# Norms, denominators and turns as single items between products; folds on ScalarE, q and k loaded from ScalarE's queue, pieces of x issued later

## The chip, the cores and the metric

The kernel runs on 1 core of a Trainium2 chip. A core has five engines with an instruction stream each: TensorE (PE in the profile; its weight loads are PEld), VectorE (DVE), ScalarE (ACT), GpSimd (POOL) and SyncE (SP), which here only issues DMAs. ScalarE issues DMAs too (rows named ACTq), from the same stream as its arithmetic. The metric is device time in microseconds (us) of the slowest core; here there is one.

## The reference

Everything is float32. Attention runs on 8 batches of 12 heads, sequence 448, head width 64; its output, with the heads side by side, is the input x of a token and channel mixer.

```python
def rmsnorm(x, g):
    rms = np.sqrt(np.mean(x * x, axis=-1, keepdims=True) + 1e-06)
    return x / rms * g
q_n, k_n = (rmsnorm(q, g_q), rmsnorm(k, g_k))
scores = scale * np.matmul(q_n, k_n.transpose(0, 1, 3, 2))
scores = scores - np.max(scores, axis=-1, keepdims=True)
attn = np.exp(scores)
attn = attn / (np.sum(attn, axis=-1, keepdims=True) + 1e-09)
x = np.matmul(attn, v)          # (8, 12, 448, 64) -> (8, 448, 768)
...
h = np.maximum(x.transpose(0, 2, 1) @ w_tok1, 0.0) @ w_tok2   # 448 -> 256 -> 448
u = x + h.transpose(0, 2, 1)
h2 = np.maximum(u @ w_ch1, 0.0) @ w_ch2                       # 768 -> 1536 -> 768
return u + h2
```

## The kernel before, in words

**Two bodies.** The product of the two gains decides at run time whether scores can be exponentiated without subtracting their maximum. The measured inputs take that body (`shifted` is false); the other is not run.

**Attention.** Two heads make a pair, six pairs a batch, 48 pairs in all; two pairs make a t, so a batch has three t. Each t has four steps, s = 0 to 3 (`att_step`). Item `tiled` of a step holds scores for one or two of seven key blocks k (L321, with one exp per pair on ScalarE, L325, from four PSUM banks s_ps), and the products with v of earlier blocks (L395, into two banks o_ps). Step 0 also finishes the t before: its last two blocks, and then `denominator` for its two pairs. For the first batch (pairs 0 to 5) the row sums are matmuls with ones (L375) into m_ps; later they are sums of the exps on POOL and VectorE (`group_sums`, L363) and one small matmul into d_ps.

`denominator` is four VectorE instructions for a pair: transpose the sums (L422), reciprocal of one column in 32 (L424), transpose back (L426), multiply o_ps into uT, the transposed x (L428).

**Norms.** q and k of a pair are squared on ScalarE (L1000, or L1005 for pairs below 12) and summed on VectorE (L1001, L1008) into ms. `roots` turns the sums of two pairs into reciprocal roots: for pairs from 12 on the two halves of a head width lie on different partitions, so four copies (L1027, the fold) and one sum (L1028) come first; then a first guess (L1036) and three Newton steps of three instructions (L1039 to L1041). `scale` multiplies q and k by them (L286, one a pair), and `turn_qk` transposes: with matmuls for pairs below 12 (`plain`, L298), otherwise on VectorE (L301); ScalarE applies the gains (L304). The buffer of q and k is one of two slots (qk_t); pair p + 2 overwrites pair p once that is turned. For pairs from 12 on, `load_qk` issues eight DMAs a pair (L983), all on SP.

**The mixer.** `tok1` (L565) needs x with the sequence on partitions. For the first batch matmuls transpose uT; for the others `trans_x` transposes a 128-column piece on VectorE into one of four buffers `turned` (`turn`, L523), sends it with four DMAs to a scratch xs in memory (`send`, L529, on SP), and after three pieces loads half of x from there (L556, on SP). `tok2` (L573) has its result added to uT by VectorE (L578). The channel products (`ch1`, L695; `ch2`, L752) go through PSUM banks m_ps, of which there are two; seven products replace eight, with sums on VectorE, POOL and ScalarE: of each seven, product i = 4 (and i = 0) is copied out by ScalarE, the others are taken out by VectorE (L700, L761). At the batch's end `turns` transposes uT again on VectorE and sends it to the output with four DMAs a piece on ScalarE's queue (L529).

**Weights.** They arrive as 8-byte numbers. `weight_items` converts them chunk by chunk (three VectorE instructions L213, L214, L216, two on ScalarE, one VectorE L233, one POOL L247) and stores them to scratch memory (ws); `sum_items` add the sums that the seven products need, on POOL. Products read units of weights from there (`load_units`, L621, on SP, six buffers, four or five ahead).

**The order.** Every engine's instructions are issued in the order in which the program is written (a manual schedule). Work is a list of items, each a planned cost in us and a function; `merge` interleaves two lists so that both are through by the same share of their planned cost at any time. In the main loop a batch's mixer (`early`) is merged with the next batch's attention (`att_items`), with `x_items` (0.1 a piece) in it. Items of planned cost 0 follow their predecessor directly, with nothing between: for later batches these are the squares of a pair (steps 0 and 1), the roots, both scalings, the turns and the loads. A product is planned at 2.24.

**Kernel start.** `Start` loads pairs 0 and 1 and norms pair 0 before the branch; pair 1 follows after it, pairs 2 and 3 after the first scores.

Of the kernel before, what the change touches and what calls it, by code (L numbers as in the profile page):

```python
# [44 lines left out]
def whole(ctx, tc, shifted, pre, q, k, v, g_q, g_k, moe_w_tok1, moe_w_tok2, moe_w_ch1, moe_w_ch2, out):  # L45
# [66 lines left out]
    s_tile = lambda name: ps_S.tile([P, 512], F32, name=name, tag="S")  # L112

# [295 lines left out]
    def denominator(p):  # L409
        b, j = divmod(p, NPAIR)  # L410
        if j == 0:
            st["uT", b] = uT_pool.tile([P, NC, S], F32, name="uT")
        ps = st.pop(("d", p))

        dt = rd_pool.tile([P, S], F32, name="dt", tag="rd")
        if shifted:
            nc.vector.tensor_scalar(dt[:], ps[:, 0:S], 1e-9, None, ALU.add)
            src = dt[:]
        else:

            src = ps[:, 0:S]
        nc.vector.transpose(out=dt[:], in_=src)  # L422
        rc = pre.nt_pool.tile([P, NB], F32, name="rc")
        nc.vector.reciprocal(out=rc[:], in_=dt[:].rearrange("p (n c) -> p n c", c=32)[:, :, 0])  # L424
        rd = rd_pool.tile([P, S], F32, name="rd", tag="rd")
        nc.vector.transpose(  # L426
            out=rd[:].rearrange("p (n c) -> p n c", c=32), in_=rc[:].unsqueeze(2).to_broadcast([P, NB, 32]))
        nc.vector.tensor_tensor(out=st["uT", b][:, j, :], in0=st.pop(("o", p))[:, 0:S], in1=rd[:], op=ALU.mult)  # L428
        st.pop(("v", p))
# [3 lines left out]
    def att_step(g):  # L433
# [8 lines left out]
        def finish():  # L442
            if s == 0 and t:
                last = (p - 2, p - 1)
                for k in (NK - 2, NK - 1):
                    values(last, k)
            if live:
                for k in ((0,), (1, 2), (3, 4), (5, 6))[s]:
                    score(t, k)
            if s == 0 and t:  # L450
                if not on_pe(p - 1):
                    row_sums(t - 1)
                for i in last:
                    denominator(i)
# [16 lines left out]
        def both_shifted():  # L471
# [8 lines left out]
            denominator(i)  # L480
# [10 lines left out]
        items.append((2.4 if s == 1 else 3.2, tiled))  # L491
        if live and not on_pe(p):
# [6 lines left out]
        if live and s in (3, 0):  # L499
            j = p + 4 if s == 3 else p + 3  # L500
            if pre.first_slot + 2 <= j < NP:
                items.append((0.0, lambda: pre.load_qk(j, st)))

        n = p + 2
        if g in (0, 3):
            n = 2 if g == 0 else 4
            items += [(0.3, lambda i=i: pre.squares(n + i, st)) for i in range(2)]
        elif live and s < 2 and NPAIR <= n < NP:
            items.append((0.0, lambda: pre.squares(n + s, st)))
        if g in (0, 3) or live and s == 1 and NPAIR <= n < NP:  # L510
            items.append((0.3 * (n < NPAIR), lambda: pre.roots(n, 2, st)))
            items += [(0.3 * (n < NPAIR), lambda i=i: scale(n + i)) for i in range(2)]
        if turned and not inside:
            items += [(0.4 * pre.plain(q), lambda i=i: turn_qk(q, i)) for i in (1, 0)]
# [18 lines left out]
    def x_tile(half):  # L533
        st["x", half] = x_pool.tile([P, NS, HC], F32, name="x")
        return st["x", half]

    def trans_x(b, j):

        half, o = divmod(j * P, HC)
        if b == 0:  # L540

            if o == 0:
                x_tile(half)
            ps = s_tile("t_ps")
            for c in range(NS):
# [3 lines left out]
                out=st["x", half][0:R, :, o:o + P], in_=ps[0:R, :].rearrange("p (c n) -> p c n", c=NS))  # L549
# [4 lines left out]
        send(nc.sync, turn(b, j), xs[:, o:o + P])  # L554
        if o + P == HC:
            nc.sync.dma_start(out=x_tile(half)[0:R], in_=xs[:].rearrange("(c p) n -> p c n", c=NS))  # L556
            st.pop(("xs", half))

    def tok1(b, jc, h):
# [4 lines left out]
        for c in range(NS):  # L564
            nc.tensor.matmul(  # L565
                out=ps[:, 0:HC], lhsT=w1_sb[0:R, c, jc * P:(jc + 1) * P], rhs=st["x", h][0:R, c, :],
# [218 lines left out]

    def turns(b, cs):

        def trans(cc):
            st["y", b, cc] = turn(b, cc)

        def sent(cc):
            send(nc.scalar, st.pop(("y", b, cc)), out[b][:, cc * P:(cc + 1) * P])

        items = [(0.3, lambda cc=cc: trans(cc)) for cc in cs]
        late = [(0.3, lambda cc=cc: sent(cc)) for cc in cs]
        return items[:2] + [it for two in zip(late, items[2:]) for it in two] + late[max(0, len(cs) - 2):]
# [49 lines left out]
    scale(0)  # L846
    turn_qk(0, 1)
    turn_qk(0, 0)
    load_v(0)
    load_v(1)  # L850
    for i in range(5):
        weight_load(i)
        if i < NPAIR - 2:
            pre.load_qk(2 + i, st)
        if i < 2:
            load_v(2 + i)
    for i in range(2):
        pre.load_qk(pre.first_slot + i, st)

    pre.squares(1, st)  # L860
    pre.roots(1, 1, st)
    scale(1)
    turn_qk(1, 1)
    turn_qk(1, 0)
# [3 lines left out]
    for _, fn in merge(  # L868
            att_items(0, 8) + merge(att_items(8, AHEAD * per + 1), x_items(0, 0)), weight_items(0, BEFORE)):
        fn()  # L870
    left, sums = [], sum_items()
    for b in range(B):
# [5 lines left out]
        else:  # L878

            for _, fn in merge(tok1_items(b, 0), left):  # L880
                fn()
# [8 lines left out]
        for _, fn in merge(att, early[:len(early) - tail]) + early[len(early) - tail:] + last_items(b, sums[6:12]):  # L890
            fn()
        left = turns(b, [2, KC + 2])
    for _, fn in left:
        fn()


class Start:


    def __init__(self, ctx, tc, q, k, g_q, g_k, w2):  # L900
# [27 lines left out]
        self.load_qk(1, self.st)  # L928
# [12 lines left out]
        nc.gpsimd.memset(self.sq[:, :, D:D + 1], D * 1e-6)  # L941

# [3 lines left out]
        self.st["rs", 0] = const.tile([P, 4 * self.NS], F32, name="rs_0")[0:self.R]  # L946
# [164 lines left out]
```

## Time and profile before

| | us |
|---|---|
| median of 3 runs | 1449.41 |
| lowest, highest | 1445.63, 1452.39 |
| profiled execution, its own time | 1447.23 |
| its span in the profile | 1445.3 |
| TensorE busy in it | 1306.8 |
| VectorE, GpSimd, ScalarE busy | 783.0, 394.1, 368.6 |

The page gives busy times over the span, the span in 40 slices of 36.1 us (a digit is the busy share in tenths; PEclk is the clock granted to TensorE, in tenths of full speed), the chain of work that ended last, the costliest groups of instructions by line, and DMA issues. Views of the trace answer further questions: waits (who waited for whom: us in total, times, longest), the timeline (start, duration, engine, line, operation, output<-inputs, number of instructions, and in brackets the idle time before and what ended it), and tables by stretches of time. Names are the program's tiles: m_ps, s_ps, o_ps, d_ps are PSUM banks; hb is a large buffer that holds early q and k at first and the mixer's hidden values later.

### The profile page before, as it was taken

How to read it: one execution, taken by the hardware profiler on the slowest of the kernel's cores; microseconds unless marked ns; L12 is line 12 of the kernel's file. 1: busy time of each engine (PE TensorE's matmuls, PEld its weight loads, DVE VectorE, ACT ScalarE, POOL GpSimd, SP SyncE). 2: the span in 40 equal slices, each digit the busy share in tenths (PEclk: the TensorE clock that was granted, in tenths of full speed). 3: DMA queues.
4: the chain of work that ended last, by engine and by line, in shares of the span. 5: the costliest groups of instructions: out<-in, count | busy, mean ns of one | idle time of the engine just before them, and what ended most of it. 6: DMA issues, size and time to landing. Idle time of an engine off the chain costs nothing.

```text
span 1445.3 us, 20543 instructions
## 1 busy us (share of the span) xinstructions
PE 1306.8 (90%) x7408; PEld 933.5 (65%) x7408; DVE 783.0 (54%) x1382; ACT 368.6 (26%) x707; POOL 394.1 (27%) x385
## 2 busy tenths in 40 slices
PE   3777995998987899999999989999999999999997
PEld 1333442454666858786676847777587847787997
DVE  5767887435662545652656446562667446533312
ACT  3555453202231023311233013320323113210110
POOL 0112232515581222311133113220333113221220
PEclk9899998999997999999999999999999999999999
DMA  9255877795978845677356746588357746467455
GB/s 193 87 167 155 240 218 191 225 228 131 265 177 230 188 116 152 145 202 175 85 156 165 170 115 158 115 211 203 72 159 177 166 121 157 111 171 180 142 172 121
DMA packets 497396, 238.87 MB, mean 165 GB/s; under 512 B 375876, under 2 KB 455876, under 8 KB 497284
## 3 DMA queue, kind: packets, MB, share of 16 engines
q1 hardware_dynamic: 407138, 226.20, 59.5%
q10 hardware_dynamic: 90018, 11.25, 5.2%
q8 instruction: 61, 1.00, 0.3%
q14 instruction: 51, 0.42, 0.1%
q0 software_dynamic: 128, 0.00, 0.0%
HBM read 197.85 MB, written 39.52 MB: 164 GB/s over the span
## 4 chain that ended last, share of the span: by engine, by line
PE 66%; DVE 11%; DMA 11%; issue 3%; SPq 2%; ACT 1%; ACTq 1%; POOL 1%; DVEq 0%; POOLq 0%
PE m_ps L695 21%; PE m_ps L752 19%; PE o_ps L395 7%; PE s_ps L321 6%; DMA unit<-ws 4%; PE m_ps L573 4%; DMA out_dram<-turned 4%; PE m_ps L565 3%; PE m_ps L676 2%; PE m_ps L658 2%; DVE qk_t L286 2%; ACTq L529 1%; DMA ws<-raw 1%; DVE raw L214 1%; SPq L529 1%
## 5 line engine op out<-in xcount | busy, mean ns | idle before, releaser
L752 PE MATMUL m_ps<-hb,unit 128*128 128x224 f32 x1764 | 349.3, 359 | 35.2 <-DMA unit<-ws 33.7
L752 PEld LDWEIGHTS m_ps<-hb,unit 128*128 128x128 f32 x1764 | 336.2, 193 | 53.6 <-issue 33.6
L325 ACT ACTIVATE e<-s_ps 128x448 f32<-128x448 f32 x336 | 156.4, 547 | 199.0 <-PE s_ps L321 199.0
L695 PE MATMUL m_ps<-tu,unit 128*128 128x224 f32 x1008 | 203.0, 356 | 4.1 <-DVE r L700 4.1
L695 PEld LDWEIGHTS m_ps<-tu,unit 128*128 128x128 f32 x1008 | 190.2, 191 | 18.2 <-DVE r L700 8.8
L395 PE MATMUL o_ps<-e,v 64*64 64x448 f32 x1316 | 153.1, 547 | 6.6 <-DVE uT L428 5.7
L695 PEld LDWEIGHTS m_ps<-uT,unit 128*128 128x128 f32 x756 | 141.5, 190 | 18.9 <-issue 6.6
L695 PE MATMUL m_ps<-uT,unit 128*128 128x224 f32 x756 | 153.3, 356 | 0.0
L321 PE MATMUL s_ps<-qkT 64*64 64x448 f32 x1260 | 144.0, 550 | 0.5 <-ACT x L548 0.5
L761 POOL TENSOR_TENSOR uT<-uT,r 128x448 f32<-128x448 f32 (+1 forms) x56 | 59.3, 1069 | 279.0 <-DVE r L761 160.8
L761 DVE TENSOR_TENSOR uT<-uT,m_ps 128x448 f32<-128x448 f32 (+1 forms) x70 | 34.0, 502 | 137.6 <-PE m_ps L752 136.6
L573 PE MATMUL m_ps<-w_sb,h 128*128 128x448 f32 x192 | 86.4, 600 | 23.3 <-DVE uT L578 21.5
L363 DVE TENSOR_TENSOR es<-es,e 128x896 f32<-128x896 f32 x84 | 97.7, 1164 | 4.7 <-ACT e L325 2.2
L395 PEld LDWEIGHTS o_ps<-e,v 64*64 64x64 f32 x1316 | 49.4, 134 | 78.3 <-issue 66.3
L565 PE MATMUL m_ps<-x,w_sb 112*128 112x384 f32 x256 | 88.6, 497 | 2.9 <-ACT h L568 2.9
L304 ACT ACTIVATE qkT<-qkT,g_t 128x448 f32<-128x448 f32 x36 | 24.1, 669 | 261.7 <-DVE qkT L301 261.7
L321 PEld LDWEIGHTS s_ps<-qkT 64*64 64x64 f32 x1260 | 44.0, 133 | 68.8 <-issue 59.5
L363 POOL TENSOR_TENSOR es<-e 128x896 f32<-128x896 f32 x21 | 44.7, 2126 | 159.3 <-ACT e L325 159.3
L578 DVE TENSOR_TENSOR uT<-uT,m_ps 128x448 f32<-128x448 f32 x48 | 29.3, 616 | 103.0 <-PE m_ps L573 103.0
L700 POOL TENSOR_TENSOR hb<-r,r 128x448 f32<-128x448 f32 x21 | 23.8, 1134 | 223.8 <-ACT r L716 155.9
L573 PEld LDWEIGHTS m_ps<-w_sb,h 128*128 128x128 f32 x192 | 38.5, 210 | 68.8 <-issue 29.7
L247 POOL TENSOR_TENSOR stage<-raw 128x512 f32<-128x512 f32 x36 | 41.6, 1156 | 138.7 <-DVE raw L233 81.7
(92 smaller groups left out, 1426.2 us busy)
## 6 DMA issues: line engine op xcount, KB each, us to landing
unit<-ws SPq DMA_DIRECT2D x318, 384.0 KB, 3.6
raw<-in_moe_w_ch_dram SPq DMA_DIRECT2D x72, 256.0 KB, 3.6
out_dram<-turned ACTq DMA_DIRECT2D x192, 56.0 KB, 3.5
v<-in_v_dram SPq DMA_DIRECT2D x94, 112.0 KB, 3.5
xs<-turned SPq DMA_DIRECT2D x168, 56.0 KB, 1.9
x<-xs SPq DMA_DIRECT2D x14, 672.0 KB, 7.5
ws<-stage SPq DMA_DIRECT2D x36, 256.0 KB, 3.8
raw<-ws SPq DMA_DIRECT2D x36, 256.0 KB, 4.1
```

The costliest lines, as they stand in the source:

```text
L247: nc.gpsimd.tensor_tensor(out=dst, in0=lo, in1=hi, op=ALU.mult)
L286: nc.vector.tensor_tensor(out=x, in0=x, in1=r.unsqueeze(2).to_broadcast(list(x.shape)), op=ALU.mult)
L321: nc.tensor.matmul(out=pss[i][rows_of(i, a), 0:S], lhsT=qkT[h, 1, k * D:(k + 1) * D], rhs=qkT[h, 0, :], start=True, stop=True)
L325: nc.scalar.activation(out=e[:, i, :], in_=pss[i][:, 0:S], func=AF.Exp)
L363: eng.tensor_tensor(out=es[:], in0=(es if k > 1 else st["e", t, 0])[:], in1=st["e", t, k][:], op=ALU.add)
L395: nc.tensor.matmul(out=st["o", p][a * D:(a + 1) * D, 0:S], lhsT=vt[rows, k * D:(k + 1) * D], rhs=e[rows, :], **kw)
L565: nc.tensor.matmul(out=ps[:, 0:HC], lhsT=w1_sb[0:R, c, jc * P:(jc + 1) * P], rhs=st["x", h][0:R, c, :], start=(c == 0), stop=(c == NS - 1))
L573: nc.tensor.matmul(out=ps[:, 0:S], lhsT=st["h1", jc][:, cc * P:(cc + 1) * P], rhs=w2_sb[:, jc].rearrange("p c r -> p (c r)"), start=(jc == ...
L578: nc.vector.tensor_tensor(out=uT, in0=uT, in1=ps[:, 0:S], op=ALU.add)
L695: nc.tensor.matmul(out=ps[:, j * HS:(j + 1) * HS], lhsT=w[:, t, j, :], rhs=m, start=(t == 0), stop=(t == KC - 1))
L752: nc.tensor.matmul(out=ps[:, j * HS:(j + 1) * HS], lhsT=st["w"](j, t), rhs=hb[:, HB[what], t, :], start=(t == 0), stop=(t == KF - 1))
L761: add = lambda e, o, x, y: e.tensor_tensor(out=o, in0=x, in1=y, op=ALU.add)
```

## The change

- **A planned clock.** `run` adds up the planned cost of the items it executes; `later(us, fn)` puts a function off until that clock has advanced by us.
- **Denominators** become items of 0.4: transpose and reciprocal for both pairs, then transpose and product for both. For the first batch ScalarE copies o_ps to uT in between, and the product reads that copy.
- **Norms** become items of 0.4: square, reduce (both pairs at step 0, for t of 2 and more), then at step 1 fold, guess, three Newton steps, two scalings. The four copies of a fold run on ScalarE, after step 1's exps.
- **Turns** of q and k become items of 0.4 each, **loads** of q and k items of 0.2 for each DMA; for pairs from 12 on all eight DMAs of a pair are issued by ScalarE.
- **Pieces of x** are sent 2.0 planned us after their transposition, and the load of half of x stands 4.5 after the last of its three; **pieces of the output** are sent 2.0 after theirs.
- **Start:** pairs 0 and 1 share one norm before the branch, with the keys of pair 1, like those of pair 0, loaded by ScalarE; pairs 2 and 3 follow right after the branch. Pairs below 12 other than pair 0 are squared in one instruction, not in two halves.

The number of matmuls is the same (3764 in the program). ScalarE's DMAs go from 195 to 485, SP's from 1115 to 825; VectorE's copies from 72 to none, ScalarE's from 74 to 152.

```diff
+    clock, pending = [0.0], []
+    def later(us, fn):
+        pending.append((clock[0] + us, fn))
+    def run(items):
+        for c, fn in items:
+            fn()
+            clock[0] += c
+            while pending and pending[0][0] <= clock[0]:
+                pending.pop(0)[1]()
...
-    def denominator(p):
+    def denominators(ps):
+        def begin(p):
...
+            nc.vector.transpose(out=dt[:], in_=src)
+            st["rc", p] = rc = pre.nt_pool.tile([P, NB], F32, name="rc")
+            nc.vector.reciprocal(out=rc[:], in_=dt[:].rearrange("p (n c) -> p n c", c=32)[:, :, 0])
+        def raw(p):
+            b, j = divmod(p, NPAIR)
+            to = st["uT", b][:, j, :]
+            nc.scalar.copy(out=to, in_=st["o", p][:, 0:S])
+            st["o", p] = to
+        def end(p):
...
+            nc.vector.transpose(
+                out=rd[:].rearrange("p (n c) -> p n c", c=32),
+                in_=st.pop(("rc", p))[:].unsqueeze(2).to_broadcast([P, NB, 32]))
+            nc.vector.tensor_tensor(out=st["uT", b][:, j, :], in0=st.pop(("o", p))[:, 0:S], in1=rd[:], op=ALU.mult)
+        parts = [lambda p=p: begin(p) for p in ps]
+        if ps[0] < NPAIR:
+            parts += [lambda p=p: raw(p) for p in ps]
+        return parts + [lambda p=p: end(p) for p in ps]
...
         items.append((2.4 if s == 1 else 3.2, tiled))
+        part = lambda fns, c=0.4: [(c, fn) for fn in fns]
+        if s == 0 and t and not shifted:
+            items += part(denominators((p - 2, p - 1)))
...
-                items.append((0.0, lambda: pre.load_qk(j, st)))
-
-        n = p + 2
-        if g in (0, 3):
-            n = 2 if g == 0 else 4
-            items += [(0.3, lambda i=i: pre.squares(n + i, st)) for i in range(2)]
-        elif live and s < 2 and NPAIR <= n < NP:
-            items.append((0.0, lambda: pre.squares(n + s, st)))
-        if g in (0, 3) or live and s == 1 and NPAIR <= n < NP:
-            items.append((0.3 * (n < NPAIR), lambda: pre.roots(n, 2, st)))
-            items += [(0.3 * (n < NPAIR), lambda i=i: scale(n + i)) for i in range(2)]
+                eng = nc.sync if pre.plain(j) else nc.scalar
+                items += part(pre.loads(j, st, eng, eng), 0.2)
+        n = p + 2 if t > 1 else p + 4
+        if live and s == 1 - (t > 1) and t != 1 and n < NP:
+            items += part([lambda i=i, f=f: f(n + i, st) for i in range(2) for f in (pre.square, pre.reduce)])
+        if live and s == 1 and t != 1 and n < NP:
+            items += part(pre.roots(n, st)) + part([lambda i=i: scale(n + i) for i in range(2)])
         if turned and not inside:
-            items += [(0.4 * pre.plain(q), lambda i=i: turn_qk(q, i)) for i in (1, 0)]
+            items += part([lambda i=i: turn_qk(q, i) for i in (1, 0)])
...
-        send(nc.sync, turn(b, j), xs[:, o:o + P])
+        t = turn(b, j)
+        later(2.0, lambda: send(nc.sync, t, xs[:, o:o + P]))
         if o + P == HC:
-            nc.sync.dma_start(out=x_tile(half)[0:R], in_=xs[:].rearrange("(c p) n -> p c n", c=NS))
             st.pop(("xs", half))
+            later(4.5, lambda: nc.sync.dma_start(
+                out=x_tile(b, half)[0:R], in_=xs[:].rearrange("(c p) n -> p c n", c=NS)))
...
+    def trans_y(b, cc):
+        t = turn(b, cc)
+        later(2.0, lambda: send(nc.scalar, t, out[b][:, cc * P:(cc + 1) * P]))
     def turns(b, cs):
...
+        return [(0.3, lambda cc=cc: trans_y(b, cc)) for cc in cs]
...
+    pre.load_qk(2, st)
+    pre.load_qk(3, st)
     load_v(0)
     load_v(1)
...
+    scale(0)
+    pre.square(2, st)
+    for p in range(2):
+        if p:
+            scale(p)
+        turn_qk(p, 1)
+        turn_qk(p, 0)
+    pre.reduce(2, st)
+    pre.square(3, st)
+    pre.reduce(3, st)
+    for part in pre.roots(2, st):
+        part()
+    scale(2)
+    scale(3)
...
-        self.load_qk(1, self.st)
+        self.load_qk(1, self.st, other=nc.scalar)
...
+            for p in range(2):
+                self.square(p, self.st)
+                self.reduce(p, self.st)
+            for part in self.roots(0, self.st):
+                part()
...
+    def fold(self, p, st):
+        x = st["ms", p + 1].rearrange("p a n -> p (a n)")
+        st["half", p] = t = self.nt_pool.tile([128, 56], F32, name="half", tag="nt")
+        for m in range(4):
+            self.nc.scalar.copy(out=t[32 * m:32 * m + 32], in_=x[32 * (m ^ 1):32 * (m ^ 1) + 32])
...
+    def roots(self, p, st):
+        parts = [] if self.plain(p) else [lambda: self.fold(p, st)]
+        return parts + [lambda: self.guess(p, st)] + [lambda i=i: self.newton(p, st, i == 2) for i in range(3)]
```

`guess` holds L1028 and L1036 of before, `newton` one round of L1039 to L1041; `square` and `reduce` hold what `squares` held.

## The prediction

> **What bounds the kernel now.** I read the page first (busy shares, 40 slices), then TensorE's own waits, then the timeline around its longest gaps, the SP queue's waits and a table by stretches.
>
> ```profile
> PE 1306.8 (90%) x7408; PEld 933.5 (65%) x7408; DVE 783.0 (54%) x1382; ACT 368.6 (26%) x707; POOL 394.1 (27%) x385
> ...
> PE   3777995998987899999999989999999999999997
> ...
> DVE  5767887435662545652656446562667446533312
> ...
> PEclk9899998999997999999999999999999999999999
> ```
>
> TensorE is the bound: 1306.8 of 1445.3 us. What is left is 138.5 us: 12.6 before the first matmul, 9.1 after the last (it ends at 1436.2), and 117 in gaps between. The change touches no matmul, so it can win only from those 117 us and from half-clock stretches. TensorE's waits say what ends the gaps (us in total, times, longest):
>
> ```profile
> PE m_ps L752 <- DMA unit<-ws: 33.7, 11, 16.0
> PE m_ps L573 <- DVE uT L578: 21.5, 7, 5.1
> PE t_ps L298 <- DVE hb L286: 19.0, 2, 12.6
> PE m_ps L676 <- DMA unit<-ws: 16.4, 1, 16.4
> PE t_ps L298 <- issue: 8.6, 1, 8.6
> PE o_ps L395 <- DVE uT L428: 5.7, 2, 5.3
> ```
>
> Two causes: VectorE late (L573, L298, L395) and a unit of weights late (L752, L676). The first in the timeline of batch 2:
>
> ```profile
> 523.91 1.31 DVE L1027 COPY nt<-ms 32x56 f32<-32x56 f32 x4
> ...
> 527.99 2.10 DVE L286 TENSOR_TENSOR qk_t<-qk_t,rs 128x896 f32<-128x896 f32 x2
> 530.00 0.61 DVE L578 TENSOR_TENSOR uT<-uT,m_ps 128x448 f32<-128x448 f32 x1
> ...
> 530.67 4.49 PE L573 MATMUL m_ps<-w_sb,h 128*128 128x448 f32 x11 [2.28 <-DVE uT L578]
> ```
>
> One norm (reduce, folds, roots, two scalings) holds VectorE from 522.80 to 530.0; the eviction L578 is behind it, and TensorE idles 2.28 us. The second cause, at the end of that batch:
>
> ```profile
> 650.99 6.65 SPq L529 DMA_DIRECT2D xs<-turned  x12
> ...
> 657.74 1.49 SPq L621 DMA_DIRECT2D unit<-ws  x2
> 659.91 0.32 SPq L556 DMA_DIRECT2D x<-xs  x1
> ...
> 662.63 4.78 PE L752 MATMUL m_ps<-hb,unit 128*128 128x224 f32 x24 [1.59 <-DMA unit<-ws]
> ```
>
> SP issues twelve pieces of x, then a load of x that waits for them, and only then the unit TensorE waits for. SP also waits on ScalarE's stores:
>
> ```profile
> SPq L621 <- DMA out_dram<-turned: 52.3, 11, 8.4
> ```
>
> These data have nothing to do with each other: in the built program each DMA waits for the one eight places before it, over SP's and ScalarE's queues together. So a late DMA on one queue holds the other.
>
> **The change part by part.** The sum stands against the profiled execution, 1447.23 us (span 1445.3 and 1.9 around it); the median, 1449.41, lies 2.2 above.
>
> 1. Start. Before, pair 0 is turned from 12.59 and pair 1 from 20.72, scores begin at 22.41. Now both norms share one chain before the branch. Pair 1's keys go out on ScalarE right behind pair 0's (end near 3.1); with 4.7 us to landing (row hb<-in_q_dram) they are there at 7.8; squares 1.2, reduce 1.24, ten short steps of 32 columns 2.2 (30.34 to 32.55), branch 0.8, scaling 1.22: pair 0 turns at 14.5 (1.9 later), pair 1 one scaling and one turn later, scores at 18.3. Gain 4; ends 0 (a late landing) and 6.4 (the whole gap before 20.72). I take -4.5, as pairs 2 and 3 are normed before they are needed.
> 2. Rest of the start. Four gaps: 2.6 at 28.1, 4.5 at 33.8, 5.3 at 55.7, 8.6 at 88.4, together 21. For 55.7, the raw copy on ScalarE (row COPY 526 ns) frees o_ps without VectorE's 2.15 us of transposes, reciprocal and product per pair; but the denominators' m_ps still waits for VectorE behind a weight piece (3.0 us: 0.43+1.34+0.53+0.70). For 88.4, the norm of pairs 6 and 7 still stands one step before its turn. Half: -10, ends 0 and -21. VectorE's work is unchanged but for the folds.
> 3. The wait at 235 (16.4). The units there come at 248.26, behind 6.2 us of pieces of x (242.0 to 248.2) and 3.6 us of q and k. Now the three transposes stand before two weight pieces, and the q and k are on ScalarE; the pieces still precede the units. -5; ends 0 (the last weights are VectorE's, whatever SP does) and -10.
> 4. Norms at tok2 (L573, 21.5 in 7 waits). Folds leave VectorE (72 copies, 37.6 us); scalings come one by one between products. At a batch's start the order is now: roots 2.7, eviction 0.62, two scalings 2.2, eviction 0.62, beside two tok2 products (3.2) and 3.3 of scores and values. The waits should nearly go. Against it: the folds stand behind four exps (4 x 0.55) in ScalarE's queue, the root's first step behind them, and output DMAs (4 x 0.61, from four in 2.45 at 512.79) now stand right before these exps. ScalarE's price of a fold lies between 0.20 (128x1 activation) and 0.53 (128x448 copy), 0.8 to 2.1 us a set; I take 1.3, four VectorE copies. -10; ends 0 and -21.5.
> 5. SP. 288 DMAs of q and k leave it (about 0.48 us each: four in 1.90 at 539.69): 138 us of issuing. L752's waits without the one at 427 sum to 17.7. At x's first half the pieces now follow the unit load of their product, with four products (9 us) of units ahead against 6 of pieces and 3.6 of landing; at the second half four pieces, a unit, eight pieces: the last two units of the batch go ahead of the eight. -13; ends 0 and -17.7. The wait at 427 (16.0): SP issues q and k until 423.9, pieces until 430.3, and units at 433.40 landing 9.2 us later. Eight loads less in front: -5; ends 0 and -10. The later load of x (7.5 us to landing) is costed at nothing: after it come three products and two tok1, 12 us against some 9; if that cover goes, tok1's second half waits the difference. Output pieces 2 us later: covered by the next product, but turned's four buffers free later, so a transposition may hold VectorE up to 2 us with one product of slack.
> 6. Clock. The table by stretches gives 0.97 for 668 to 838 and 0.98 for 838 to 1001 (10 and 6.5 us at half clock), 0.87 for 14 to 120. Fewer gaps: -6; ends 0 and -20.
> 7. New waits. ScalarE takes the 288 DMAs, for 36 pairs. Beside an ACT eviction this goes wrong: after product i=4, copy 0.53, seven loads 3.5, relu 0.58, the eighth load, square 0.96: 6.1 us. The second square needs that load landed (5.1 plus 2.6) and ends at 8.7, reduce 9.8, two sums on VectorE 11.1, eviction of i=6 11.7. TensorE runs two products (2.28 each), scores and values (2.6), one product more: it is at 9.5 and needs that bank. 2.2 us lost. Of a batch's three steps one has this order; in the others the loads start right after the exps and the cover holds. 6 x 2.2 = +13; ends 0 and +40 (all 18 steps).
>
> Sum: -4.5 -10 -5 -10 -13 -5 -6 +13 = -40.5: 1406.7, and 1409 beside the median; I give 1408.
>
> The Trainium skill (DMA: Bandwidth & Descriptors, section "Issuing engines are not separate DMA queues") speaks against step 5: a second issuing queue saves only the sequencer's issue time, usually small beside the DMA. The rows show the issue time larger than the landing: 6.65 us for twelve against 1.9. By the rule step 5 would be near 0 and the sum 1425.
>
> The skill (TensorE: Matmul & The Clock Gate, "What's actually happening") lets the clock fall after an idle window of about 3.4 us. By it the gaps of 1.6 to 2.8 us in the batches cost no clock, step 6 would be about -3, the sum 1410; the stretch 690 to 700 shows 0.83 beside a gap of 2.7.
>
> **The rivals.**
> - A, the next wait takes over. VectorE is busy 112 of 130 us from 120 to 250, so a TensorE that arrives earlier waits longer at 235, and steps 1 and 2 are given back; x's twelve pieces remain in one bunch. Against: from 14 to 120 VectorE is busy only 73 of 106, so it too can move forward. With 1, 2 and 3 gone and half of 5: 1447.2 - 10 - 9 - 6 + 13 = 1435.
> - B, slower: ScalarE's queue becomes what TensorE waits for. Each of 36 loads of a pair holds exps, relus and copies for 4 us, more when one of eight DMAs before it is late (ACTq needs 17.30 us for 16 stores at 655.30). ScalarE's 26% busy speaks against, two banks of m_ps for it. It decides where a load costs over 1.5 us (53.5/36); at 2 us each the time is 1447 - 53.5 + 72 = 1466.
> - C, all of it: steps 1 to 6 at two thirds of their far ends (107 us, so -71), step 7 at 0: 1376. The gaps' causes are few and the change meets each; against it, step 2's and 3's VectorE work stays.
>
> **How the numbers follow.** Forecast 0.58, A 0.22, B 0.10, C 0.10. No change is within 0.5% (7 us), about what can be told here. Slower by more: B but for its mild part, 0.08. Within: B's mild part and A's upper edge, 0.06. Faster: 0.86. The range leaves out most of B and the lower half of C, and takes in A: 1376 to 1440; the forecast's own is 1390 to 1425.
>
> **What would show it.** Right: L573's and L752's waits together under 20 us; scores beginning near 18; SP with some 825 DMAs; the L395 wait on L428 gone. Step 7: TensorE waits in L695 on an eviction behind L1001, about 2 us once a batch. Wrong if L321, L395 or m_ps wait for ACT by tens of us (B), or the waits at 235 and 427 grow past 16 (A).

## The result, and the profile after

The changed kernel takes 1496.63 us (median of 4 runs, 1493.87 to 1498.27), beside 1449.07 for the kernel before on the same chip: ratio 1.0326, 95% interval 1.0296 to 1.0357. That is 47 us slower; 1408 was forecast. The profiled execution of the kernel after took 1495.31 us (span 1493.5).

The page of the kernel after, busy times and the 40 slices (37.3 us each):

```profile
PE 1331.5 (89%) x7408; PEld 945.8 (63%) x7408; DVE 801.9 (54%) x1300; ACT 390.4 (26%) x774; POOL 400.8 (27%) x385
...
PE   3969978978688988999899998998999989998997
...
PEclk9988989989699999999999999999999999999999
```

The same 7408 matmul records take 24.7 us more than before (five slices are granted a clock below 9 tenths, three before), and the gaps between matmuls sum to 136.4 us where they were 116.8. Both together are 44 of the 48 us of span; the first matmul is 3.6 later. TensorE's waits in the kernel after (us in total, times, longest):

```profile
PE s_ps L334 <- ACT qkT L317: 28.2, 9, 9.9
PE m_ps L729 <- DVE hb L734: 25.2, 5, 10.1
PE m_ps L599 <- ACT h L602: 19.7, 6, 5.8
...
PE m_ps L607 <- DVE uT L612: 8.7, 7, 2.3
PE m_ps L599 <- DMA x<-xs: 7.8, 1, 7.8
PE m_ps L786 <- DVE r L734: 6.1, 1, 6.1
```

The waits that the prediction wanted gone are gone or small: tok2 on its eviction (now L607) 8.7 instead of 21.5, none left on a unit of weights. Three others stand at the head, and all three lead back to ScalarE: the gains applied to qkT (L317), the evictions L734 (VectorE's, behind a reduction that waits for ScalarE's square), the relu of tok1 (L602; 2.9 us before). Where they arise shows in the time from each batch's first tok1 matmul to the next (us, from the records of L565 and L599; the first column is from the first matmul on, the last to the last matmul):

| kernel | start | 0 | 1 | 2 | 3 | 4 | 5 | 6 | 7 |
|---|---|---|---|---|---|---|---|---|---|
| before | 105.0 | 201.3 | 188.7 | 159.6 | 167.6 | 165.7 | 160.1 | 158.3 | 117.3 |
| after | 100.4 | 197.8 | 213.3 | 169.5 | 166.8 | 167.6 | 169.1 | 160.4 | 123.0 |

25 us are lost in batch 1, while weights are still being converted, and 28 in batches 2 to 7; start and batch 0 gain 8. The timeline of the kernel after in batch 1 (start, duration, engine, line, operation, count, in brackets the idle time before and what ended it; SPq and ACTq are the queues' DMA issues):

```profile
361.40 5.61 SPq L211 DMA_DIRECT2D ws<-raw  x4
361.41 10.38 ACTq L1022 DMA_DIRECT2D qk_t<-in_q_dram  x4
...
372.12 3.48 ACTq L1022 DMA_DIRECT2D qk_t<-in_k_dram  x3
...
375.65 0.58 ACT L735 ACTIVATE hb<-hb 128x448 f32<-128x448 f32 x1 [16.58 <-DMA qk_t<-in_q_dram]
376.52 0.32 ACTq L1022 DMA_DIRECT2D qk_t<-in_k_dram  x1
376.89 0.67 ACT L317 ACTIVATE qkT<-qkT,g_t 128x448 f32<-128x448 f32 x1 [0.66 <-DMA raw<-ws]
...
377.61 1.01 PE L334 MATMUL s_ps<-qkT 64*64 64x448 f32 x2 [9.89 <-ACT qkT L317]
```

Eight loads hold ScalarE from 361.4 to 376.8. Issuing them takes 0.32 to 0.49 us each; the rest is waiting. The records behind that view say for what: each DMA's record has the semaphore that its queue waits for first (S) and the one that it signals at its landing.

```
start  us    queue   DMA           waits for   signals
361.41 0.38  ScalarE qk_t<-in_q    S116        116
363.14 0.36  SP      ws<-raw       S114        107
365.44 0.33  ScalarE qk_t<-in_q    S107        107
366.65 0.36  SP      ws<-raw       S114        111
367.66 0.51  SP      raw<-ws       S107        113
369.12 0.32  ScalarE qk_t<-in_q    S111        111
371.47 0.32  ScalarE qk_t<-in_q    S113        113
```

A load on ScalarE waits for the landing of the DMA that last used its semaphore, eight places before in the order of the program, and that is a weight store or reload on SP, itself waiting for GpSimd (S114). Summed over the changed kernel's 288 loads: 129 us of issuing and 139 us of such waits, together 7.4 us a pair; a pair's waits are 9.0 us in batch 0, 7.3 in batch 1 and 1.9 to 2.7 later.

The second half of the cause shows once in each of batches 1 to 5 (here batch 4):

```profile
915.01 1.94 ACTq L1022 DMA_DIRECT2D qk_t<-in_q_dram  x4
...
916.99 2.56 ACTq L1022 DMA_DIRECT2D qk_t<-in_k_dram  x3
...
919.62 0.46 ACTq L1022 DMA_DIRECT2D qk_t<-in_k_dram  x1
920.12 0.95 ACT L1041 ACTIVATE sq<-qk_t 128x896 f32<-128x896 f32 x1
...
924.82 0.95 ACT L1041 ACTIVATE sq<-qk_t 128x896 f32<-128x896 f32 x1 [3.74 <-DMA qk_t<-in_k_dram]
...
925.80 1.09 DVE L1055 TENSOR_REDUCE ms<-sq 128x28 f32<-128x896 f32 x1 [3.61 <-ACT sq L1041]
...
927.87 0.62 DVE L734 TENSOR_TENSOR hb<-m_ps,r 128x448 f32<-128x448 f32 x1
...
928.54 4.22 PE L729 MATMUL m_ps<-uT,unit 128*128 128x224 f32 x12 [4.15 <-DVE hb L734]
```

The second square needs the loads just issued, so ScalarE idles 3.74 us until they land; the reduction, and behind it the eviction L734, stand in VectorE's queue until 927.87; TensorE loses 4.15 us (10.1 in batch 1, 3.5 to 3.7 in batches 2, 3 and 5). This is the order of step 7, which priced it at 2.2.

### The profile page after: what moved, and what is told of

It reads as the page before. It is cut to its first block, busy times and chain, and to the rows that moved or that the text cites. A ratio compares the mean times of both kernels' runs of the same rounds, so it can differ in the third digit from the quotient of the medians.

```text
span 1493.5 us, 20465 instructions
## 1 busy us (share of the span) xinstructions
PE 1331.5 (89%) x7408; PEld 945.8 (63%) x7408; DVE 801.9 (54%) x1300; ACT 390.4 (26%) x774; POOL 400.8 (27%) x385
## 4 chain that ended last, share of the span: by engine, by line
PE 56%; DMA 15%; DVE 4%; issue 2%; ACTq 2%; POOL 2%; ACT 2%; SPq 0%; DVEq 0%; POOLq 0%
PE m_ps L786 20%; PE m_ps L729 16%; PE s_ps L334 6%; PE o_ps L408 5%; DMA qk_t<-in_k_dram 4%; DMA out_dram<-turned 4%; DMA unit<-ws 3%; PE m_ps L607 3%; PE m_ps L599 3%; PE m_ps L710 2%; ACTq L561 1%; DMA qk_t<-in_q_dram 1%; DMA raw<-ws 1%; DMA v<-in_v_dram 1%; PE d_ps L388 1%
## 5 line engine op out<-in xcount | busy, mean ns | idle before, releaser
L786 PE MATMUL m_ps<-hb,unit 128*128 128x224 f32 x1764 | 345.0, 357 | 8.7 <-DVE r L734 6.1
L334 PE MATMUL s_ps<-qkT 64*64 64x448 f32 x1260 | 160.7, 567 | 38.5 <-ACT qkT L317 28.2
L729 PE MATMUL m_ps<-uT,unit 128*128 128x224 f32 x756 | 162.7, 371 | 28.7 <-DVE hb L734 25.2
L729 PEld LDWEIGHTS m_ps<-uT,unit 128*128 128x128 f32 x756 | 148.4, 200 | 43.7 <-DVE hb L734 26.9
L599 PE MATMUL m_ps<-x,w_sb 112*128 112x384 f32 x256 | 97.8, 536 | 28.1 <-ACT h L602 19.7
L1055 DVE TENSOR_REDUCE ms<-sq 128x28 f32<-128x896 f32 (+2 forms) x49 | 53.9, 1102 | 104.6 <-ACT sq L1041 98.5
L376 DVE TENSOR_TENSOR es<-es,e 128x896 f32<-128x896 f32 x84 | 103.2, 1228 | 6.6 <-ACT e L338 2.5
L734 DVE TENSOR_TENSOR r<-m_ps,r 128x448 f32<-128x448 f32 x63 | 39.0, 619 | 111.5 <-PE m_ps L729 85.4
L599 PEld LDWEIGHTS m_ps<-x,w_sb 112*128 112x128 f32 x256 | 51.9, 208 | 71.4 <-ACT h L602 24.1
L734 POOL TENSOR_TENSOR hb<-r,r 128x448 f32<-128x448 f32 x21 | 24.1, 1150 | 237.6 <-ACT r L750 208.5
L607 PE MATMUL m_ps<-w_sb,h 128*128 128x448 f32 x192 | 79.7, 558 | 8.7 <-DVE uT L612 8.7
L795 DVE TENSOR_TENSOR uT<-uT,m_ps 128x448 f32<-128x448 f32 (+1 forms) x70 | 33.8, 499 | 96.4 <-PE m_ps L786 96.3
L260 POOL TENSOR_TENSOR stage<-raw 128x512 f32<-128x512 f32 x36 | 41.7, 1158 | 161.9 <-DVE raw L246 67.6
```

Source lines behind the costliest of these rows:

```text
L260: nc.gpsimd.tensor_tensor(out=dst, in0=lo, in1=hi, op=ALU.mult)
L334: nc.tensor.matmul(out=pss[i][rows_of(i, a), 0:S], lhsT=qkT[h, 1, k * D:(k + 1) * D], rhs=qkT[h, 0, :], start=True, stop=True)
L376: eng.tensor_tensor(out=es[:], in0=(es if k > 1 else st["e", t, 0])[:], in1=st["e", t, k][:], op=ALU.add)
L599: nc.tensor.matmul(out=ps[:, 0:HC], lhsT=w1_sb[0:R, c, jc * P:(jc + 1) * P], rhs=st["x", b, h][0:R, c, :], start=(c == 0), stop=(c == NS - 1))
L607: nc.tensor.matmul(out=ps[:, 0:S], lhsT=st["h1", jc][:, cc * P:(cc + 1) * P], rhs=w2_sb[:, jc].rearrange("p c r -> p (c r)"), start=(jc == ...
L729: nc.tensor.matmul(out=ps[:, j * HS:(j + 1) * HS], lhsT=w[:, t, j, :], rhs=m, start=(t == 0), stop=(t == KC - 1))
```

## The experiments

All times are medians with the ratio to the kernel before on the same chip; where two kernels ran on different chips the ratios are compared, and one per cent is 14.5 us.

| run | loads on | median | ratio, 95% interval |
|---|---|---|---|
| after | ScalarE | 1496.6 | 1.0326 (1.0296 to 1.0357) |
| e1 loads back | SP | 1431.5 | 0.9875 (0.9845 to 0.9904) |
| e2 output sends back | ScalarE | 1478.6 | 1.0204 (1.0165 to 1.0243) |
| e3 before, loads moved alone | ScalarE | 1476.2 | 1.0172 (1.0134 to 1.0210) |
| e4 squares apart | ScalarE | 1471.5 | 1.0137 (1.0097 to 1.0178) |
| e5 e1 + output sends back | SP | 1417.8 | 0.9767 (0.9744 to 0.9789) |
| e6 e1 + squares apart | SP | 1437.1 | 0.9896 (0.9867 to 0.9925) |
| e7 e1 + folds back | SP | 1423.9 | 0.9824 (0.9799 to 0.9849) |
| e8 e1 + x at once | SP | 1449.3 | 0.9988 (0.9972 to 1.0004) |
| e9 = e1 + e5 + e7 | SP | 1408.9 | 0.9731 (0.9708 to 0.9755) |
| e10 = e9 + squares apart | SP | 1415.8 | 0.9786 (0.9756 to 0.9816) |
| e11 before, x later alone | SP | 1434.2 | 0.9914 (0.9888 to 0.9941) |
| e12 = e10, loads put back | ScalarE | 1443.1 | 0.9963 (0.9943 to 0.9983) |
| e13 = e10 + ScalarE work | SP | 1413.0 | 0.9756 (0.9730 to 0.9783) |
| e14 = e1 + ScalarE work | SP | 1438.0 | 0.9917 (0.9891 to 0.9943) |
| e15 = e9, squares apart early | SP | 1394.1 | 0.9621 (0.9591 to 0.9651) |

### Is it the loads?

e1 undoes the move of the loads alone:

```diff
-                eng = nc.sync if pre.plain(j) else nc.scalar
+                eng = nc.sync
```

> The changed kernel with the loads of later queries and keys issued from SP again, all else kept. Theory L (these loads hold ScalarE: in the profile after, ten us for four loads at 361.41, and the waits s_ps<-qkT 28.2 and m_ps<-hb 25.2 stand behind them): 30 to 42 us of the 47 come back, 1455 to 1467, and the gaps of 9.9 at 367.7 and 10.1 at 393.6 are gone. Theory O (the output pieces, issued 2 us later, hold ScalarE at the turn of a batch; 18 us for sixteen at 519.83): no more than 10 come back, 1487 to 1497.

1431.5: 65 us come back, more than theory L asked, and the rest of the change is 18 us faster than before. TensorE's waits of e1 (the first is the time before the first matmul):

```profile
PE t_ps L311 <- DMA raw<-in_moe_w_tok_dram: 16.7, 1, 16.7
PE m_ps L710 <- DMA unit<-ws: 13.2, 1, 13.2
PE m_ps L599 <- ACT h L602: 13.1, 6, 4.5
PE m_ps L607 <- DVE uT L612: 11.4, 12, 2.4
...
PE m_ps L786 <- DMA unit<-ws: 9.9, 2, 9.2
```

The waits for qkT and hb behind ScalarE are out of the first places (hb is left with 4.3), and three waits for units, 23 us in all, are back: that is what relieving SP had really bought. On SP the loads wait for an earlier DMA only 16 us in all, in four waits (139 us on ScalarE); and where they wait for their buffer, which VectorE's turns free (82.7 us over 18 waits of SP), nobody but later transfers stands behind them.

e3 makes the same move in the kernel before:

```diff
-                items.append((0.0, lambda: pre.load_qk(j, st)))
+                items.append((0.0, lambda: pre.load_qk(j, st, act=not pre.plain(j))))
...
-            eng = other or self.nc.sync if i else self.nc.sync
+            eng = self.nc.scalar if act else other or self.nc.sync if i else self.nc.sync
```

> The kernel before, with the loads of later queries and keys issued from ScalarE and nothing else changed (eight in one item, not eight items). Theory L: 20 to 45 us slower than before, 1470 to 1495, with TensorE waiting for qkT and hb around 360 to 400. Theory O: within 7 of before, 1442 to 1456.

1476.2, 25 us slower than before. Theory L holds, but only 25 of the 65 belong to the loads alone. In the profiled execution 20 us of the loss lie in batch 1 (208.8 us, 188.7 before) and 3 in batch 0, while weights are still being stored; batches 2 to 7 take 927.0, and took 928.6. The wait that appears in e3 is the one of the kernel after:

```profile
PE s_ps L321 <- ACT qkT L304: 27.2, 8, 9.7
```

### What makes 25 into 65?

e4 keeps the loads on ScalarE and moves the second square (and its reduction) away from them, to where it was:

```diff
-        if live and s == 1 - (t > 1) and t != 1 and n < NP:
-            items += part([lambda i=i, f=f: f(n + i, st) for i in range(2) for f in (pre.square, pre.reduce)])
+        if live and s < 2 and t != 1 and n < NP:
+            who = (s,) if t > 1 else (0, 1) if s else ()
+            items += part([lambda i=i, f=f: f(n + i, st) for i in who for f in (pre.square, pre.reduce)])
```

> The changed kernel with the second pair's square and reduction one step later, as before, so that they don't stand behind their own pair's loads; the loads stay on ScalarE. Theory S (it is not the issue of the loads but the square behind them that holds ScalarE and VectorE: sq<-qk_t 102.0 and ms<-sq 98.5): 10 to 25 us come back, 1472 to 1487. Theory L (the issue itself holds ScalarE): within 6 of the changed kernel, 1490 to 1503.

1471.5: 27 us come back, a little past theory S. Its waits:

```profile
PE s_ps L334 <- ACT qkT L317: 37.2, 8, 8.6
PE m_ps L600 <- DMA out_dram<-turned: 20.3, 4, 5.6
...
PE m_ps L730 <- DVE hb L735: 6.3, 2, 6.2
```

The wait on the eviction behind the reduction falls from 25.2 to 6.3. The wait on qkT, which stands behind the loads, doesn't: it was 28.2. So the two parts have each their wait. (The second line is tok1's wait behind the output pieces; see e2.) e6 makes the same edit with the loads on SP (e1's edit and e4's):

> Loads on SP, and the second pair's square and reduction one step later, as before. Theory S (a square right behind its own loads costs on any queue, since ScalarE waits for their landing): 5 to 12 us faster than 1431.5. Theory Q (with the loads on SP they land in time, and the square costs only where it stands on the queue that issues them): within 5 of it, 1427 to 1436.

1437.1: nothing gained, 3 us (by the ratios) to 6 lost (the intervals of e1 and e6 overlap). Theory Q holds for the whole: a square right behind its loads costs 27 us when it stands on the queue that issues them, and nothing on balance where another queue issues them. ScalarE's idle time before its squares, as far as the landing of keys ends it (issuing and waits of the loads included), says the same, in the kernel after and in e1:

```profile
ACT sq L1041 <- DMA qk_t<-in_k_dram: 102.0, 23, 15.6
...
ACT sq L1041 <- DMA qk_t<-in_k_dram: 9.3, 2, 6.3
```

But the times of the batches, as in the table above, show that e6's nothing is a gain and a loss that cancel:

| kernel | start | 0 | 1 | 2 | 3 | 4 | 5 | 6 | 7 |
|---|---|---|---|---|---|---|---|---|---|
| e1 | 101.5 | 192.3 | 188.5 | 161.3 | 160.0 | 159.6 | 158.2 | 159.3 | 122.2 |
| e6 | 96.4 | 184.0 | 184.1 | 159.9 | 168.5 | 164.3 | 166.0 | 161.7 | 123.6 |
| e4 | 95.3 | 186.0 | 192.5 | 166.7 | 170.0 | 168.8 | 173.3 | 160.8 | 122.3 |

Up to batch 2 e6 gains 19 us over e1, and then it loses 25. The same edit gains e4 40 us over the kernel after up to batch 2, and then loses 8. So the later square has a gain and a price of its own; what the queue adds to it is the difference of the two edits, 30 us by the ratios.

The 65 us are then 27 (the square), 35 (the loads with the squares apart, e4 against e6) and 3. Beside the 26 of e12, below, the 35 leave some 9 for loads that share ScalarE with folds and delayed output pieces, which is no more than the intervals allow.

### Is it the issuing, or the waiting?

e12 has the edits of e4, e5 and e7 below, e10 that of e1 too: they differ in the loads alone.

> The changed kernel with output pieces sent at once, folds on VectorE and the second square later, but with the loads still on ScalarE: the run with four parts undone, with the loads alone put back. Theory L (the loads on ScalarE cost by themselves, about 35 as between the two runs with the later square, 1471.5 and 1437.1): 25 to 40 us slower than the run with four parts undone. Theory V (they cost mainly because squares, folds and output pieces stand beside them on ScalarE): under 15 us slower than it.

1443.1 against 1415.8: 26 us by the ratios, theory L; it is e3's price again. Theory V falls. The wait on qkT is 36.8 us in e12 and not in e10's list. ScalarE is held as long as in the kernel after (127 us of issuing, 134 of waits); what differs is what stands behind.

e13 and e14 keep the loads on SP and give ScalarE work of the length of the issuing, at the same places:

```diff
+    def spend(self):
+        for _ in range(2):
+            self.nc.scalar.copy(out=self.warm[:], in_=self.warm[:])
...
-                items += part(pre.loads(j, st, eng, eng), 0.2)
+                more = lambda: None if pre.plain(j) else pre.spend()
+                items += part([lambda f=f: (f(), more()) for f in pre.loads(j, st, eng, eng)], 0.2)
```

> The run with four parts undone (loads on SP, 1415.8), with sixteen tiny ScalarE copies a pair (about 3.6 us, the length of issuing eight loads) where the loads are issued, in place in a tile that nothing else reads. The loads on ScalarE cost 27 here. Theory I (the issue's length is the price): 15 to 30 us slower, 1431 to 1446. Theory W (the price is the waits for earlier DMAs in ScalarE's queue): under 10 slower, 1414 to 1426.

> The changed kernel with its loads on SP (1431.5) and the same sixteen ScalarE copies a pair where the loads are issued. The loads on ScalarE cost 65 here, with the second square right behind them. Theory I: 40 to 65 us slower, 1471 to 1497. Theory W: under 20 slower, 1431 to 1451.

e13 takes 1413.0 (e10: 1415.8, no difference), e14 1438.0, 6 us over e1 by the ratios (their intervals overlap). The row of this work in e13:

```profile
L1011 ACT COPY warm<-warm x576: 173/192/219, 198.5 to 1186.6; 128x1 f32<-128x1 f32 x192
```

576 copies of 0.192 us are 111 us, beside 129 of issuing. Theory W: ScalarE has room for the time of issuing, which costs 0 of 26 and 6 of 65. What is left as the price is the waits: the loads' own, for earlier DMAs, and the square's, for the landing. The landing is later too: a load of keys takes 4.3 us to it by the median in the kernel after and 2.7 in e1, and why stays open. Not tried was a kernel with the loads on ScalarE and semaphores that SP's DMAs don't share; so that the sharing by itself makes the waits is read from the records, not from a run.

### The other parts

e2 (loads on ScalarE) and e5 (on SP) send the pieces of the output as before, one item after their turn:

```diff
-        later(2.0, lambda: send(nc.scalar, t, out[b][:, cc * P:(cc + 1) * P]))
...
-        return [(0.3, lambda cc=cc: trans_y(b, cc)) for cc in cs]
+        items = [(0.3, lambda cc=cc: trans(cc)) for cc in cs]
+        late = [(0.3, lambda cc=cc: sent(cc)) for cc in cs]
+        return items[:2] + [it for two in zip(late, items[2:]) for it in two] + late[max(0, len(cs) - 2):]
```

> The changed kernel with the output pieces sent as before (one item after their turn, no delay), all else kept. Theory O: the five waits of TensorE for the first relu of tok1 (m_ps<-h, 19.7 in 6) go, 15 to 20 us come back: 1476 to 1482. Theory L: within 5 of the changed kernel, 1492 to 1502.

> The changed kernel with the loads on SP (the run that took 1431.5) and the output pieces sent as before. Theory O (the delay of the output pieces costs by itself: waits m_ps<-h of 13.1 in that run, and 4.9 us more than before after the last tok1): 12 to 18 us faster than that run, 1414 to 1420. Theory P (the delay costs only beside loads on ScalarE): within 5 of it, 1427 to 1436.

18 us come back in e2, 16 in e5: theory O both times, and the price is the same with and without the loads (theory P falls). The kernel after at the start of batch 2 shows why:

```profile
519.83 18.36 ACTq L561 DMA_DIRECT2D out_dram<-turned  x16
...
527.67 5.33 PE L599 MATMUL m_ps<-x,w_sb 112*128 112x384 f32 x16
...
538.23 0.49 ACT L602 ACTIVATE h<-m_ps 128x384 f32<-128x384 f32 x1 [27.42 <-DMA out_dram<-turned]
...
538.78 3.57 PE L599 MATMUL m_ps<-x,w_sb 112*128 112x384 f32 x5 [5.79 <-ACT h L602]
```

Sixteen DMAs (four pieces) need 18.4 us of ScalarE's queue, and tok1, which began at 527.7, waits for the relu behind them. In the kernel before, at the start of batch 3:

```profile
655.30 17.30 ACTq L529 DMA_DIRECT2D out_dram<-turned  x16
...
667.24 5.33 PE L565 MATMUL m_ps<-x,w_sb 112*128 112x384 f32 x16
...
673.20 2.20 PE L565 MATMUL m_ps<-x,w_sb 112*128 112x384 f32 x6 [0.63 <-ACT h L568]
```

Sixteen DMAs took 17.30 us here too, but began 11.9 us ahead of tok1 instead of 7.8, and TensorE lost 0.6 us.

e7 puts the folds back on VectorE, with the loads on SP:

```diff
-            self.nc.scalar.copy(out=t[32 * m:32 * m + 32], in_=x[32 * (m ^ 1):32 * (m ^ 1) + 32])
+            self.nc.vector.tensor_copy(out=t[32 * m:32 * m + 32], in_=x[32 * (m ^ 1):32 * (m ^ 1) + 32])
```

> Loads on SP, and the folds back on VectorE (four copies a set, 37.6 us in all before). Theory F (the folds' move is what took the norm out of the way of the evictions at tok2): 6 to 14 us slower than 1431.5, with the wait m_ps<-uT behind tok2 back toward 21. Theory I (it is the splitting into items that did it): within 5 of 1431.5.

1423.9, 7 us faster: neither theory had the sign. Tok2's wait is

```profile
PE m_ps L607 <- DVE uT L612: 4.2, 5, 2.0
```

against 11.4 in e1. On ScalarE a fold comes after four exps, and VectorE's next step waits for it (L1072 on L1063, 104.1 us in e1), with evictions queued behind. So the folds' move cost, and it did not take the norm out of tok2's way. The splitting into items did not do it alone either: e9 and e10, below, both have it, with the folds on VectorE, and differ only in the place of the second square. Their waits at tok2:

```profile
PE m_ps L607 <- DVE uT L612: 6.1, 4, 2.4
...
PE m_ps L608 <- DVE uT L613: 18.5, 7, 3.7
```

With the square in its later place, as before the change, the wait is nearly back at 21.5.

e8 issues x's pieces and loads at once, with the loads on SP; e11 gives the kernel before the delay of x and nothing else.

```diff
-        later(2.0, lambda: send(nc.sync, t, xs[:, o:o + P]))
+        send(nc.sync, t, xs[:, o:o + P])
...
-            later(4.5, lambda: nc.sync.dma_start(
-                out=x_tile(b, half)[0:R], in_=xs[:].rearrange("(c p) n -> p c n", c=NS)))
+            nc.sync.dma_start(out=x_tile(b, half)[0:R], in_=xs[:].rearrange("(c p) n -> p c n", c=NS))
```

> Loads on SP, and the pieces and loads of x issued at once, as before. Theory X (the delay lets units go ahead of x's pieces, which took the waits for units, 33.7, away): 5 to 13 us slower than 1431.5, with unit<-ws waits back in every batch. Theory Y (the delay did nothing): within 5 of it.

> The kernel before, with the delay of x's pieces and loads and nothing else of the change. Theory X (the delay by itself lets the units past x's pieces): 10 to 20 us faster than before, 1431 to 1442, with unit<-ws waits of TensorE under 25 in all instead of 50. Theory Y (the delay counts only where the norms no longer hold VectorE): within 7 of before, 1444 to 1458.

e8 loses 16 us, more than theory X asked, and e11 gains 12, as it asked. By its waits the theory is less plain, and its bound of 25 was missed: in e8 unit<-ws is 22.3 in 8 plus 13.3, in e11 still 36.4 in 12 plus 8.0. Of e11's 12 us, the fall of these waits from 50.1 to 44.4 explains 6; its gaps in all go from 116.8 to 105.3. Its gain lies in batch 0 (190.6 us, 201.3 before).

### Together

e9 has the edits of e1, e5 and e7.

> The changed kernel with three parts undone: loads on SP, output pieces sent at once, folds on VectorE. Theory M (the three costs stand at different places and add up): 1431.5 - 13.7 - 7.6 = 1410, between 1405 and 1415. Theory N (they are the same slack at the turn of a batch): 1415 to 1424, as the better single one.

1408.9: the three costs add up (theory M). Then the square's place, whose two prices e10 (e9 with the edit of e4) and e15 tell apart:

> As the run with three parts undone, and the second pair's square one step later as well. Theory T (what the later square lost with the loads on SP was the wait for the first relu, 27.5, which the output pieces cause; without it its gain at the start, 5 us to the first tok1 and 8 in the next batch, is left): 1394 to 1406. Theory U (the later square costs by itself in the steady batches): 1412 to 1422.

> Three parts undone (1408.9) and the second square one step later in the first nine double pairs only. By the stages of the two runs the early part gains 4 + 7 + 6 us and the late part keeps what it had: 1390 to 1396 (theory T). If the later square's price moves with it to the next stage: 1403 to 1412 (theory U).

e10 loses 7 us to e9 (theory U). Its times from tok1 to tok1, as in the table of batches, say where: 97.0, 185.0, 181.2 at first (e9: 101.2, 192.2, 187.4), then 164.5, 158.4, 161.9, 163.2 (e9: 160.4, 154.6, 156.9, 155.6). e15 takes the later square only for t below 9:

```diff
+            who = (s,) if 1 < t < 9 else (0, 1) if s == 1 - (t > 1) else ()
```

1394.1, ratio 0.9621, theory T: faster than both kernels, 55 us under the one before. Its page:

```profile
PE 1296.6 (93%) x7408; PEld 929.6 (67%) x7408; DVE 817.0 (59%) x1372; ACT 373.0 (27%) x702; POOL 403.9 (29%) x385
```

Apart from the time before the first matmul (16.5), its two largest waits are for units of weights while these are still being made, 13.8 in 2 and 11.5 in 1. Why the later square helps early was not settled; in the later batches the wait that it lengthens most is tok2's on its eviction, shown above.

## Why the prediction was wrong, by its steps

The ladder: kernel before, -39 us for what is good in the change (e9), +21 for folds and output pieces (e9 to e1), +65 for the loads: +47. Of the 89 us between forecast and result, step 7 makes 52 (13 priced, 65 paid). The other steps make 36: priced at -53.5 together, they are worth -18 in e1.

1. Start, -4.5: scores begin at 19.35, not 18.3, 3.1 earlier than before; but the first tok1 comes at 116.6 (117.6 before). The gain was given back at 26.05, at the next turn:

```profile
24.59 2.36 DVE L299 TENSOR_TENSOR hb<-hb,rs 112x1024 f32<-112x1024 f32 x2
...
28.57 0.72 ACT L237 ACTIVATE e_t<-e_t,expo_c 112x512 uint32<-112x512 uint32 x1 [3.87 <-DVE e_t L229]
...
32.36 1.81 ACT L338 ACTIVATE e<-s_ps 128x448 f32<-128x448 f32 x4
...
32.93 1.38 PE L311 MATMUL t_ps<-ident,hb 112*128 112x112 f32 x6 [6.88 <-ACT e L338]
```

The scalings of the next pairs now hold VectorE just before a weight piece; ScalarE's part of that piece waits 3.87 us, and exps stand behind it. "Normed before they are needed" did not look at what else they would hold.

2. The rest of the start, -10: nothing. The gaps at 26.0, 74.0, 82.0, 102.4 and 109.3 sum to 20.4 us, the four before were 21.
3. The wait at 235, -5: 13.2 in e1 (16.4 before), -3, inside its ends.
4. Tok2, -10: right in size (21.5 to 8.7), wrong in its cause. It named the folds, which cost 7 (e7), and the scalings as single items; with both of these but the square in its old place the wait is 15.8 (e6), and with the earlier square 11.4 (e1). So the size came out right by a part that the step did not name, which was luck.
5. SP relieved, -18: the waits for units went, as said, but paid elsewhere. What stays when the loads return to SP is the delay of x, worth 12 to 16 (e8, e11): the step named the later pieces among the reasons of its -13 and costed the later load at nothing. That load's cover did go once: tok1 waits 7.8 us for x in the kernel after. The delay of the output pieces, also costed at nothing, cost 16 to 18; the cover named, the next product, covers VectorE's buffers, and the piece's place in ScalarE's queue ahead of tok1's relus was not counted.
6. Clock, -6: TensorE's busy time rose 24.7 us with the new gaps and fell 10.2 in e15 without them. The granted clock is one half for 126 us of the kernel after between its first matmul and its last, for 96 before and for 68 in e15. The sign follows the gaps; of the 24.7 us, half clock explains some 15 (half of 30), and the rest was not traced. Short gaps can go with it: in the kernel before the clock is one half for 3.4 us right behind gaps of 2.0 to 2.7 us (from 394, 694, 861, 994 and 1186 on).
7. New waits, +13 with ends 0 and +40: +65. This is the step that failed. It counted ScalarE's time for a load as issuing (4 us a pair; 3.6 measured), which e13 shows to cost nothing, and left out, without a reason, 139 us of waits for DMAs eight places before, though the first part of the prediction had told of that coupling as something that SP suffers. With the loads on ScalarE, it is ScalarE that suffers it. The order behind the square was in the right place, and was priced at 2.2 where it cost 3.5 to 10.1.

Rival B had the mechanism and its condition ("more when one of eight DMAs before is late"), priced it at 1466 with 2 us a pair, and got 0.10. Its 2 us were near (65 us over 36 pairs are 1.8); what kept it 30 us too low were the gains of 53.5 that it took over from the forecast. ScalarE's 26% busy spoke against it, and that was a poor reason: the records of the kernel before had shown ACTq at 17.3 us for sixteen stores.

On the Trainium skill's rule that a second issuing queue saves only the issue time (DMA: Bandwidth & Descriptors, "Issuing engines are not separate DMA queues"): the move saved SP's issuing and took away 23 us of waits for units, so the near 0 that the prediction worked out from the rule was too small a gain; the whole was a loss of 25 to 65 us, which the rule does not speak of. The prediction held against the rule that issue time is larger than the landing, but it set the issue of twelve DMAs (6.65 us) beside the landing of one (1.9); one beside one it is 0.55 to 1.9, which agrees with the rule's "usually small". The same page says (section "Anatomy of one DMA — SWDGE (gpsimd) path", told there beside GpSimd's path) that a DMA's semaphore wait happens on the issuing sequencer before dispatch; the 139 us that ScalarE spent so, and the 16 on SP, agree.

## What to carry to other kernels

Before a DMA moves to a compute engine's queue, list what it may wait for (its buffer, its data, and the DMA whose semaphore it reuses) and what stands behind it on that engine; the issue time was the least of it here. A busy share says how much work an engine has, not how long it may be held. And undo a change part by part before it is judged: here good parts worth 39 us were hidden under bad ones worth 86.

## What was not expected of the hardware

- 111 us of extra ScalarE work, spread where the loads were, cost 0 and 6 us (e13, e14), while 139 us of waits spread over the same places came with 25 us and more. Work of fixed length in small pieces was hidden; the waits came in lumps (fifteen over 1 us in batch 0, the longest 4.9). That the lumps make the difference is likely, but no run shows it.
- Putting transfers off can gain by itself: x's pieces 2 and x's load 4.5 planned us later gave the kernel before 12 us (e11).
- The same edit, a square one step later, gained 18 us in the first three stages and lost 20 in the next four (e9, e10).
